# A hedgehog linear-attention and SwiGLU block: a rewrite with TensorE transposes, token-major q and k, kv summed on the fly, a folded output sum and one order of TensorE work

## Chip, cores, metric

One core of a Trainium2 chip. The metric is the device time of one execution in microseconds (us), lower is better. Engines are named as in the profile: PE is TensorE (PEld its weight loads), DVE VectorE, ACT ScalarE, POOL GpSimd, SP the engine that issues most DMAs.

## The reference, cut

```python
# x: 2048 tokens x 640, bf16; 32 heads of 20; FFN width 1728
q, k, v = split_heads(x @ wqkv)
pq, pk  = q @ w_phi[h], k @ w_phi[h]                # per head, 20 x 20
phi_q   = concat(softmax(pq), softmax(-pq))         # 40 features per head
phi_k   = concat(softmax(pk), softmax(-pk))
kv      = sum over tokens of phi_k^T v              # 40 x 20 per head
z       = sum over tokens of phi_k                  # 40 per head
a       = (phi_q @ kv / (phi_q @ z + 1e-6)) @ wo
b       = (silu(x @ w_gate) * (x @ w_up)) @ w_down
g       = sigmoid((x * gate_w).sum(-1))
out     = g * a + (1 - g) * b
```

q needs kv and z of all tokens, so the k side must end before any attention output. The FFN depends on nothing of this and can fill TensorE meanwhile. Both kernels first multiply wq and wk by w_phi, so that pq and pk are one product each.

## The kernel before, the parts that matter

A helper records every operation, keeps for each address range who wrote and read it last, and emits the semaphore waits. It also makes an engine wait for its own earlier instruction where ranges conflict; a PSUM address counts as its whole bank.

```python
def req(ev):                      # in run(): what an instruction must wait for
    ...
    s, v = ev
    if v > need.get(s, 0):
        need[s] = v               # also where s is the engine's own semaphore
...
for c in range(5):                # x and wq, wk are transposed by the DMA
    dma("sp", xT[:, c, :], x2[:, c * P:(c + 1) * P], transpose=True)
...
def tile_k(t):                    # token-major: 128 tokens x 640
    mm_group(p1(b, "pk0"), [(xT[:, c, tok], wqk[:, 1, c, 0:512]) for c in range(5)])
    mm_group(p1(b, "pk1"), [(xT[:, c, tok], wqk[:, 1, c, 512:D]) for c in range(5)])
    # ACT: exp(+), exp(-); DVE: sums, reciprocals; POOL: scale. ek kept for all tokens
...
def kv_group(c, sg):              # after all k tiles: 12 groups of 16 matmuls, 126 columns
    pairs = [(ek[:, sg, t, 120 * c:120 * c + nr], v1[:, t, 126 * c:126 * c + ncol]) for t in range(NT)]
...
def zw_groups(bt, buf):           # normaliser sums, q feature-major: 8 groups of 6 matmuls, one bank
    for u in range(4):
        for sg in range(2):
            oap = ps[0:P, c0: c0 + 64]
            ...
            mm_group(oap, pairs)
...
def u_loop(bt, buf):              # 512 tokens: wo into its own banks, w_down into others
    mm_group(bank(ab0, 0, 512), pairsa0)        # 6 chunks
    mm_group(bank(ab1, 0, P), pairsa1)
    mm_group(bank(4, 0, 512), pairs0)           # 14 chunks
    mm_group(bank(5, 0, P), pairs1)
    actop(aga, a_ap, ACTF.Copy, scale=gcol)     # g * a
    dveop(...)                                  # (1 - g) * b + that
```

The normalising factors of q are worked out token-major, transposed on PE, and spread to features again by 48 further matmuls of 512 columns.

The softmax here doesn't subtract the row's maximum and nothing guards it: scores larger than these inputs give would overflow.

## Time and profile before

The median is 377.19 us (377.03 to 378.57, 4 runs). The profiled execution spans 376.0 us.

First the busy table of the page of the kernel before (engine, busy us, share of the span, instructions), then the two lines of its chain of work that ended last (shares of the span by engine, then by line).

```profile
PE 340.0 (90%) x2164; PEld 178.1 (47%) x2201; DVE 139.2 (37%) x258; ACT 156.9 (42%) x290; POOL 127.9 (34%) x153
PE 84%; ACT 4%; SPq 3%; DVE 3%; issue 2%; DMA 2%; POOLq 0%; POOL 0%
PE ps L310 83%; SPq L297 3%; DMA xT<-in_A_x_dram 2%; ACT eq L325 2%; DVE ksum L471 1%; DVE hT L621 1%; PE pst L316 1%; ACT hT L325 1%; ACT oT L325 1%; ACT wqk L325 0%; ACT us L325 0%; POOLq L797 0%; DVE krec L472 0%; POOL hT L624 0%; DVE ocomb L661 0%
...
```

PE is what the kernel waits for. How close it is to its own limit is read from the timeline, where each line is a start, a length, the engine, the operation, the shape and a count; a length can reach past the next start (1.24 us from 93.81, the next start at 94.89), so rates are read from start to next start. The view of the kernel before, PE only:

```profile
92.04 1.93 PE L310 MATMUL ps<-v_55,ek 128*120 128x126 bf16 x32
93.81 1.24 PE L310 MATMUL ps<-xT,wg 128*128 128x512 bf16 x5
94.89 1.24 PE L310 MATMUL ps<-xT,wu 128*128 128x512 bf16 x5
...
174.84 3.22 PE L310 MATMUL ps<-SZW,eq 120*128 120x64 bf16 x48
178.12 1.02 PE L310 MATMUL ps<-xT,wg 128*128 128x512 bf16 x4
```

Five matmuls of 512 columns take 1.08 us (93.81 to 94.89), 216 ns each. The 32 of 126 columns take 1.77 us, 55 ns each. Columns / 2.4 GHz + 2.5 ns fits both (215.8 and 55.0 ns). It is a fit to these timings, and the streamed times below are estimates made with it. The 48 normaliser matmuls of 64 columns take 3.28 us, 68 ns each, where that sum gives 29: here something holds PE.

The waits of PE in the kernel before, longest first (total, times, longest):

```profile
PE ps L310 <- DMA xT<-in_A_x_dram: 20.0, 1, 20.0
...
```

By the program's own count PE streams 764,112 columns in 2,201 matmuls: 318.4 us for the columns and 5.5 for the 2.5 ns each, 324 us. The other 52 us of the span are no work of PE.

### The profile page before, as it was taken

The page shows a single profiled execution, that of the slowest core. Times are in us where ns is not written, and L with a number is a line of the kernel's source. Part 1 is how long each engine was busy: PE and PEld are TensorE (multiplying, and loading weights), DVE is VectorE, ACT ScalarE, POOL GpSimd, SP SyncE. Part 2 cuts the span into 40 slices and gives each one's busy share as a digit, 9 for nine tenths or more (in the row PEclk, how much of TensorE's full clock was granted, in tenths as well). Part 3 has the DMA queues.
Part 4 walks back from the last instruction along what each step waited for, and adds up shares of the span by engine and source line. Part 5 has one row for each costly group of instructions (what it writes and reads, how often), then busy time and mean ns, then how long its engine had stood idle before and what let it go on. Part 6 is the DMA issues. An engine that isn't in the chain of part 4 may idle for free.

```text
span 376.0 us, 5517 instructions
## 1 busy us (share of the span) xinstructions
PE 340.0 (90%) x2164; PEld 178.1 (47%) x2201; DVE 139.2 (37%) x258; ACT 156.9 (42%) x290; POOL 127.9 (34%) x153
## 2 busy tenths in 40 slices
PE   0088899999999998999999999999999999999996
PEld 0044455557654543554444455444445554444454
DVE  1000898883321580112772201157420111782211
ACT  0134666672357445113537213634551154436210
POOL 4970698784262120003333200214340012333200
PEclk9999999999999999999999999999999999999999
DMA  8968766200000000000000011000000100000011
GB/s 181 186 133 184 244 169 187 61 0 2 2 0 2 0 2 0 30 24 21 0 0 1 2 37 35 0 2 0 2 0 19 35 17 2 1 2 0 2 35 37
DMA packets 29510, 15.54 MB, mean 41 GB/s; under 512 B 19309, under 2 KB 29485, under 8 KB 29485
## 3 DMA queue, kind: packets, MB, share of 16 engines
q1 hardware_dynamic: 27097, 14.34, 15.5%
q10 hardware_dynamic: 1812, 0.83, 1.0%
q8 instruction: 18, 0.29, 0.3%
q0 software_dynamic: 576, 0.01, 0.1%
q14 instruction: 7, 0.06, 0.0%
HBM read 8.30 MB, written 2.62 MB: 29 GB/s over the span
## 4 chain that ended last, share of the span: by engine, by line
PE 84%; ACT 4%; SPq 3%; DVE 3%; issue 2%; DMA 2%; POOLq 0%; POOL 0%
PE ps L310 83%; SPq L297 3%; DMA xT<-in_A_x_dram 2%; ACT eq L325 2%; DVE ksum L471 1%; DVE hT L621 1%; PE pst L316 1%; ACT hT L325 1%; ACT oT L325 1%; ACT wqk L325 0%; ACT us L325 0%; POOLq L797 0%; DVE krec L472 0%; POOL hT L624 0%; DVE ocomb L661 0%
## 5 line engine op out<-in xcount | busy, mean ns | idle before, releaser
L624 POOL TENSOR_TENSOR hT<-hT,us 128x512 bf16<-128x512 bf16 (+1 forms) x56 | 64.3, 1151 | 200.0 <-DVE hT L621 104.6
L621 DVE SCALAR_TENSOR_TENSOR hT<-hT,ps 128x512 bf16<-128x512 bf16 (+1 forms) x56 | 38.0, 684 | 86.6 <-ACT hT L325 86.6
L310 PE MATMUL ps<-xT,wu 128*128 128x512 bf16 (+1 forms) x273 | 69.0, 379 | 0.4
L310 PE MATMUL ps<-xT,wg 128*128 128x512 bf16 (+1 forms) x269 | 67.3, 379 | 2.0 <-DVE hT L621 1.1
L310 PE MATMUL ps<-wd,hT 128*128 128x128 bf16 (+1 forms) x440 | 62.5, 297 | 1.2 <-POOL hT L624 0.9
L325 ACT ACTIVATE hT<-ps 128x512 bf16<-128x512 f32 (+1 forms) x56 | 33.3, 595 | 49.5 <-PE ps L310 49.5
L310 PEld LDWEIGHTS ps<-wd,hT 128*128 128x128 bf16 x448 | 35.0, 98 | 27.2 <-POOL hT L624 0.8
L474 POOL TENSOR_TENSOR ek<-ek,krec 128x640 bf16<-128x640 bf16 x32 | 39.7, 1268 | 19.0 <-ACT ek L325 14.6
L310 PE MATMUL ps<-wvg,xT 128*128 128x500 bf16 (+1 forms) x160 | 26.2, 316 | 20.9 <-DMA xT<-in_A_x_dram 20.0
L661 DVE SCALAR_TENSOR_TENSOR ocomb<-ps,gs,ag 128x640 bf16<-128x640 f32 x16 | 14.1, 884 | 82.6 <-PE ps L310 82.6
L325 ACT ACTIVATE us<-ps 128x512 bf16<-128x512 f32 (+1 forms) x56 | 33.5, 598 | 26.5 <-PE ps L310 26.1
L310 PEld LDWEIGHTS ps<-xT,wu 128*128 128x128 bf16 (+1 forms) x280 | 27.0, 99 | 32.4 <-issue 2.8
L310 PEld LDWEIGHTS ps<-xT,wg 128*128 128x128 bf16 (+1 forms) x280 | 25.9, 98 | 31.1 <-PE ps L310 2.9
L325 ACT ACTIVATE ag<-ps,gs 128x640 bf16<-128x640 f32 x16 | 12.7, 793 | 62.4 <-PE ps L310 62.4
L471 DVE TENSOR_REDUCE ksum<-ek 128x32 f32<-128x640 bf16 x32 | 25.1, 783 | 36.1 <-ACT ek L325 36.1
L325 ACT ACTIVATE eq<-ps 120x512 bf16<-120x512 f32 (+1 forms) x48 | 26.0, 593 | 20.8 <-PE ps L310 20.5
L588 DVE TENSOR_TENSOR eq<-eq,ps 120x512 bf16<-120x512 bf16 (+1 forms) x48 | 30.7, 681 | 3.6 <-PE ps L310 3.4
L310 PE MATMUL ps<-wo,oT 120*128 120x512 bf16 (+3 forms) x188 | 28.6, 297 | 1.3 <-ACT oT L325 0.7
L310 PE MATMUL ps<-xT,wqk 128*120 128x512 bf16 (+1 forms) x120 | 29.3, 380 | 0.2 <-DVE hT L621 0.2
L310 PEld LDWEIGHTS ps<-wvg,xT 128*128 128x128 bf16 x160 | 14.3, 102 | 32.2 <-issue 22.4
L325 ACT ACTIVATE ek<-ps 128x640 bf16<-128x640 f32 x32 | 20.8, 701 | 11.4 <-PE ps L310 11.3
L310 PE MATMUL ps<-wqk,xT 128*128 128x128 bf16 (+1 forms) x154 | 23.2, 296 | 1.1 <-ACT wqk L325 0.8
(59 smaller groups left out, 246.6 us busy)
## 6 DMA issues: line engine op xcount, KB each, us to landing
out_dram<-ocomb SPq DMA_DIRECT2D x16, 160.0 KB, 1.8
wg<-in_B_w_gate_dram SPq DMA_DIRECT2D x4, 540.0 KB, 3.8
wu<-in_B_w_up_dram SPq DMA_DIRECT2D x4, 540.0 KB, 3.9
wd<-in_B_w_down_dram SPq DMA_DIRECT2D x1, 2080.0 KB, 13.3
wvg<-in_A_wqkv_dram ACTq DMA_DIRECT2D x1, 800.0 KB, 6.8
wo<-in_A_wo_dram SPq DMA_DIRECT2D x1, 750.0 KB, 6.8
wbd<-in_A_w_phi_dram ACTq DMA_DIRECT2D x14, 0.8 KB
wbd<-in_A_w_phi_dram POOLq DMA_DIRECT2D x14, 0.8 KB, 6.1
```

The lines of the kernel that those rows point to most:

```text
L297: return eobj.dma_start(dst, src, transpose=True)
L310: last = pe.matmul(out_ap, lhsT=l, rhs=r, start=(i == 0), stop=(i == n - 1))
L316: return pe.transpose(out_ap, in_ap, ident[:, :])
L325: return act.activation(out_ap, in_ap, func, scale=scale)
L471: dveop(lambda eka=eka, sa=sa: dve.tensor_reduce(sa, eka, AX.X, ALU.add), [eka], [sa])
L474: poolop(lambda eka=eka, rb=rb: pool.tensor_tensor(eka, eka, rb, ALU.mult), [eka, ra], [eka])
L588: dveop(lambda ea=ea, oap=oap: dve.tensor_tensor(ea, ea, oap, ALU.mult), [ea, oap], [ea])
L621: dveop(lambda hap=hap, gap=gap: dve.scalar_tensor_tensor(out=hap, in0=hap, scalar=1.0, in1=gap, op0=ALU.add, op1=ALU.mult), [hap, gap], [ ...
L624: poolop(lambda hap=hap, usa=usa: pool.tensor_tensor(hap, hap, usa, ALU.mult), [hap, usa], [hap])
L661: dveop(lambda oc=oc, b_ap=b_ap, omg=omg, aga=aga: dve.scalar_tensor_tensor(out=oc, in0=b_ap, scalar=omg, in1=aga, op0=ALU.mult, op1=ALU.add),
```

## The change

The intent: fewer columns through PE, and PE never waiting. The new kernel is a rewrite; the core of the diff, with cuts:

```diff
@@ the helper: PE no longer waits for itself
+            if s == eng and not dma and (eng == "pe" or not raw):
+                return
...
@@ inputs: plain loads, transposed on PE, copied out by DVE
-    for c in range(5):
-        dma("sp", xT[:, c, :], x2[:, c * P:(c + 1) * P], transpose=True)
+    def xpose(t0, n):
+        ...
+            transposes([(o[:, c * P:(c + 1) * P], xs[:, t % 6, c * P:(c + 1) * P]) for c in range(5)])
+            copy("dve", xT[:, t, :, :].rearrange("p c k -> p (c k)"), o)
...
@@ the v weights first, the gate's column of 640 elements after them into the same tile
+    dma("act", wvg[:, :, 0:D], wv_src)
+        dma("pool", wvg[:, :, D:D + 1], bass.AP(gate_w.tensor, gate_w.offset, [[1, P], [P, 5], [1, 1]]))
...
@@ kv: one tile after the other into two banks that stay open, 11 chunks of 3 heads x 2 signs
+    def kvtile(t):
+        for j in range(NCH):
+            o = bank(bk, 63 * jj, 63 * jj + 63, 0, 120)
+            pairs.append((o, ekr[:, b, 120 * j:120 * j + 120], v1r[:, b, 63 * j:63 * j + 63], ...))
...
@@ q token-major; normalisers by DVE; the scaled features transposed by the DMA
-    def zw_groups(bt, buf):        # and zw_ops, zw_transposes, exp_psi_item
+    def qtile(t):
+        pr = tok_proj(t, 0)
+        head_exps(pr, e)
+        def vec():                 # nine vector operations, recorded one item later
+            reduce(qz[:, s, :], e.rearrange("p (g d) -> p g d", d=DH))
+            tt("dve", ez[:, s, :], e, zb[:, 0:1280], ALU.mult)
+            reduce(qw[:, s, :], ez[:, s, :].rearrange("p (g d) -> p g d", d=DH))
+            ...                    # five small ones, up to the factors qc, times g / (1 - g)
+            tt("pool", ...)        # ph = eq * qc
+            dma("sp", phiT[:, (t // 4) % 2, t % 4, :, :], ph[:, b, :], transpose=True)
+        defer(1, vec)
+    def oitem(bt, part):           # 64-row products in pairs: partitions 0 to 63, and 64 to 127
+                    l, o = kvsb[0:120, j, :], bank(2 * pr + i, 0, 512, 64 * s, 64 * s + 64)
...
@@ w_down and wo in one accumulation, scaled once by 1 - g
+        ls = [(hT[:, buf, k, tok], wd[:, k, :]) for k in range(13)]
+        ls += [(hT[0:104, buf, 13, tok], wd[0:104, 13, :])]
+        ls += [(oT[:, buf, m, tok], wog[:, m, :]) for m in range(5)]
+        actop(o.rearrange("p (b c) -> p b c", b=2), halves(pr), ACTF.Copy, omg[:, t:t + 1])
...
@@ every piece of PE work gets a place in one order; each takes the next of 3, later 4, pairs of PSUM banks
+    for u in range(4):
+        put(NT + 3.65 + 1.6 * u, qtile, u)
+    todo.sort(key=lambda z: z[:2])
```

The items also put the instructions for DVE, ACT and POOL into the program, so the order of items is the order of their instructions too.

## The prediction

> **What bounds the kernel now.** TensorE. The page's busy table has PE at 340 of 376 us; the chain of waits puts 83% of the span on it. The timeline gives its rate: groups of five 128x512 matmuls start 1.08 us apart (216 ns each), 32 of 126 columns take 1.77 us (55 ns each), 28 alternating 512/128 3.80 us. That is columns/2.4 GHz + 2.5 ns[...]; weight loads never show as a limit. The program streams 764,000 columns in 2,205 matmuls: 318 + 6 = 324 us (estimate). The other 52 us: PE waits 20.0 us for transposed x; 3 us of tail (fused DVE op, output DMA); about 29 us of holes: the first k tiles waiting for ACT and DVE (37 to 46 us), normaliser groups of six 64-column matmuls that wait for each other in one bank (3.3 us per block against 1.5 streamed), small PE transposes, ACT waits at 142 to 146 us.
>
> **What the change does to PE.** Gone, in columns: normaliser sums (12k), expansion of the factors (25k), padding of the q projection (10k) and of wo (10k), dense premultiply (24k, becomes 7k), kv at 126 columns (21.5k, becomes 11k), half-empty FFN chunks (10k). Down-projection and wo share one accumulation: 5.16 us per token tile against 5.44. Added: 130 transposes of 128 columns (17k), a 1.3k broadcast. New total 683,000 columns in about 2,040 matmuls: 285 + 5 = 290 us, 34 us less, all on the critical path. Two terms are uncertain by 4 us each: the 63-column kv matmuls may be held by their 120-column weight loads (at most 55 ns, against 29 streamed), and the paired 64-row output matmuls in different array halves may overlap ([...]no run here yet shows it).
>
> **Start.** x arrives untransposed. But the first v tile needs the gate column, whose DMA waits for all of wv and goes through POOL's queue (before: wv 6.8 us, small POOL DMAs 6 us to landing). I expect the first v matmul at 11 to 12 us and the first k matmul near 24 (36.9 before). PE still loses about 14 us there.
>
> **Other engines.** ACT stays near 160 us. DVE grows from 139 to about 175: 48 reductions of 1280 (about 1.4 us, from 783 ns for 640), about 4.7 us per q tile in all. POOL: 128 to about 150 (1280-wide scaling, about 2.5 us). None passes PE. Vector work of q delays the FFN's DVE op by up to 5 us, about what four PSUM pairs hide. 16 DMA transposes have 15 us of slack. The last four x tiles queue behind all FFN weights and land near 54 us, needed near 51: 0 to 5 us lost.
>
> **Sum.** 290 + 2 (terms above) + 14 start + 2 cold clock + 3 tail + 6 holes = **317 us**, range **308 to 331**. Faster by over 2%: 0.96; within 2%: 0.03; slower: 0.01.
>
> **Right or wrong shows in:** PE busy about 300; first v matmul at 11 to 12 us; no PE wait over 1 us between 60 us and the end; five-matmul FFN groups still 1.08 us apart; down group 5.16 us.
>
> **Wrong if:** PE waits for DVE in the q stretches (325 and up); kv or transposes run above 60 ns; x tiles 12 to 15 arrive late; the granted clock falls under 0.9; or the start is under 8 us (310).

The rate is the fit above. That weight loads are no limit is what the chain of the kernel before shows: PEld is on none of its lines, though busy for 47% of the span. The 2 us for the cold clock have their measure in the same trace: the 500-column v matmuls of the kernel before start about 415 ns apart from 20.0 to 24.3 us, and 211 ns apart from there on; 4.3 us at about half the rate lose about 2 us (estimate). The 15 us of slack of the DMA transposes is the author's estimate; in the new kernel one took 3.5 us from issue to landing (median of 16).

## The result and the profile after

326.12 us median (325.45 to 327.81, 4 runs) against 377.19 us. The ratio is 0.8646, 95% interval 0.8619 to 0.8672. Ratios here and below are the mean time of one kernel's fast runs over that of the other's of the same rounds, so not quite the ratio of the medians quoted.

The profiled execution of the new kernel is the slowest of the four (327.81 us; its span of 326.1 us is close to the median of the device times only by accident, the other three spans are 323.7 to 324.6). Its mean clock is 0.990, that of the others 0.995 or 1.0. So the sums below, which are made on this span, hold about 2 us that the other executions don't have.

Of the new kernel, the busy table and the chain of the page:

```profile
PE 301.0 (92%) x2041; PEld 182.5 (56%) x2041; DVE 177.5 (54%) x266; ACT 151.4 (46%) x254; POOL 153.4 (47%) x117
PE 80%; DVE 9%; ACT 4%; DMA 4%; POOL 1%; issue 1%; POOLq 0%
PE ps L252 79%; DMA wvg<-in_gate_w_dram 2%; DVE qw L291 2%; DVE qz L291 2%; DVE ez L280 2%; DMA wvg<-in_A_wqkv_dram 2%; PE ps L264 2%; POOL ekr L280 1%; DVE hT L284 1%; DVE ksum L291 1%; ACT wqk L270 1%; ACT ekr L270 1%; ACT eq L270 1%; DVE qd L294 0%; ACT v1r L270 0%
...
```

PE still leads, but DVE now has 9% of the chain. The waits of PE in the new kernel:

```profile
PE ps L264 <- DMA xs<-in_A_x_dram: 7.0, 4, 3.4
PE ps L252 <- DVE hT L284: 6.4, 4, 2.5
PE ps L252 <- DMA wvg<-in_gate_w_dram: 2.8, 1, 2.8
PE ps L252 <- POOL ekr L280: 2.3, 2, 1.5
...
```

The waits for x and the gate are the start. The 6.4 us for DVE were not in the forecast's sum in that size. The timeline of the new kernel, PE only, at the first v tiles, the first k tiles, a kv group, the q stretch and one steady output tile:

```profile
12.67 4.38 PE L252 MATMUL ps<-wvg,xT 128*128 128x320 bf16 x20 [2.82 <-DMA wvg<-in_gate_w_dram]
16.89 0.72 PE L264 MATMUL ps<-ident,xs 128*128 128x128 bf16 x10
...
26.19 4.45 PE L252 MATMUL ps<-wqk,xT 128*128 128x320 bf16 x20 [1.30 <-ACT wqk L270]
30.47 0.44 PE L264 MATMUL ps<-ident,wqn 128*128 128x128 bf16 x5
...
43.77 0.74 PE L252 MATMUL ps<-v1r,ekr 128*120 128x63 bf16 x11
44.35 1.53 PE L252 MATMUL ps<-wvg,xT 128*128 128x320 bf16 x10
...
125.63 1.25 PE L252 MATMUL ps<-xT,wg 128*128 128x512 bf16 x5 [2.50 <-DVE hT L284]
...
141.71 1.67 PE L252 MATMUL ps<-phiT,kvsb 120*64 120x512 bf16 x7 [1.85 <-DVE hT L284]
143.31 2.30 PE L252 MATMUL ps<-xT,wg 128*128 128x512 bf16 x5
...
160.88 3.97 PE L252 MATMUL ps<-wd,hT 128*128 128x320 bf16 x28
164.68 1.52 PE L252 MATMUL ps<-wog,oT 128*128 128x320 bf16 x10
166.04 1.24 PE L252 MATMUL ps<-xT,wg 128*128 128x512 bf16 x5
...
179.93 1.05 PE L252 MATMUL ps<-phiT,kvsb 120*64 120x512 bf16 x8
180.92 1.25 PE L252 MATMUL ps<-xT,wt 128*128 128x512 bf16 x5
```

Read from start to start: an output tile takes 5.16 us (160.88 to 166.04), exactly its 38 matmuls of 320 columns at full rate. A kv group of 11 takes 0.58 us (43.77 to 44.35), 53 ns for 63 columns that would stream in 29. Twenty v matmuls take 4.22 us at the start (12.67 to 16.89) where full rate is 2.72: the trace has them 267 ns apart up to 15.6 us and 136 ns apart from 15.8, so the clock is not yet up. Twenty matmuls of the first k tile take 4.28 us (26.19 to 30.47), again 267 ns apart up to 29.4 us and 136 from there. PE waits 2.50 and 1.85 us for DVE before 125.63 and 141.71, and five matmuls at 143.31 take 2.1 us (to the next start, not shown) in place of 1.08: after the second wait the clock fell. The trace's record of the granted clock has two such drops in this execution, 25.98 to 29.40 and 142.04 to 145.45 us, 3.4 us each at half.

Why the longer wait left the clock alone and the shorter one did not, the record does not show. In this execution its changes lie at 3, 4, 37, 38 and 91 times 3.413 us from its first entry (15.74 us). Cut into such stretches, the wait of 1.85 us lay whole in one (138.62 to 142.04), and the clock was at half in the next; the wait of 2.50 us (123.13 to 125.63) was cut by the border at 124.97 into 1.84 and 0.66. But PE was busy 1.57 us in the stretch before the drop and also 1.57 us in that from 121.56 to 124.97, after which none came. And in the reordered run (run 5) the same wait of 1.85 us, 139.39 to 141.24, left the clock alone: the five matmuls after it take 1.09 us (142.38 to 143.47), and the mean clock is 1.000. So the length of the wait does not decide it alone; a threshold is not shown.

The windows view of the new kernel (stretch, its length, then busy us and instruction count of PE, PEld, DVE, ACT and POOL, granted clock, DMA share, GB/s), for the q stretch and one after it:

```profile
103.00:146.00 43.00, 37.55 (x190) 17.80 (x188) 39.69 (x56) 25.20 (x42) 29.15 (x18) 0.96 0.21 40
146.00:200.00 54.00, 54.00 (x334) 31.71 (x332) 23.52 (x37) 23.41 (x38) 21.83 (x16) 1.00 0.15 35
```

From 146 us to the last matmul PE has no listed wait. In the q stretch DVE is busy 39.7 of 43 us.

### Where the 51 us came from

"Streamed" is columns / 2.4 GHz + 2.5 ns a matmul by the program; "lost until the first k matmul" is its start less what PE streamed before it (36.90 less 12.76; 26.19 less 10.09).

| | before | new |
|---|---|---|
| streamed | 323.9 | 289.9 |
| lost until the first k matmul | 24.1 | 16.1 |
| after the last matmul | 3.0 | 3.6 |
| everything else | 25.0 | 16.5 |
| span | 376.0 | 326.1 |

Two thirds of the gain are columns not streamed (34 us), 8 us the start. Of "everything else" before, the first run below shows that some 10 us were PE waiting for itself.

### The profile page after: what moved, and what is told of

Read it like the earlier page. It is cut to its first block, busy times and chain, and to the rows that moved or that the text cites. A ratio compares the mean times of both kernels' runs of the same rounds, so it can differ in the third digit from the quotient of the medians.

```text
span 326.1 us, 4990 instructions
## 1 busy us (share of the span) xinstructions
PE 301.0 (92%) x2041; PEld 182.5 (56%) x2041; DVE 177.5 (54%) x266; ACT 151.4 (46%) x254; POOL 153.4 (47%) x117
## 4 chain that ended last, share of the span: by engine, by line
PE 80%; DVE 9%; ACT 4%; DMA 4%; POOL 1%; issue 1%; POOLq 0%
PE ps L252 79%; DMA wvg<-in_gate_w_dram 2%; DVE qw L291 2%; DVE qz L291 2%; DVE ez L280 2%; DMA wvg<-in_A_wqkv_dram 2%; PE ps L264 2%; POOL ekr L280 1%; DVE hT L284 1%; DVE ksum L291 1%; ACT wqk L270 1%; ACT ekr L270 1%; ACT eq L270 1%; DVE qd L294 0%; ACT v1r L270 0%
## 5 line engine op out<-in xcount | busy, mean ns | idle before, releaser
L252 PE MATMUL ps<-xT,wg 128*128 128x512 bf16 x260 | 65.7, 384 | 4.0 <-DVE hT L284 3.6
L280 POOL TENSOR_TENSOR ph<-eq,qc 128x1320 bf16<-128x1320 bf16 x16 | 38.8, 2425 | 58.9 <-DVE qc L533 58.9
L252 PE MATMUL ps<-xT,wu 128*128 128x512 bf16 x260 | 64.6, 379 | 0.0
L270 ACT ACTIVATE hT<-ps 128x512 bf16<-128x512 f32 (+2 forms) x60 | 35.8, 596 | 60.0 <-PE ps L252 55.9
L252 PE MATMUL ps<-wd,hT 128*128 128x320 bf16 x448 | 63.5, 299 | 0.0
L280 POOL TENSOR_TENSOR ekr<-ekr,krec 128x1280 bf16<-128x1280 bf16 x16 | 37.6, 2357 | 34.5 <-DVE krec L294 34.5
L252 PE MATMUL ps<-wqk,xT 128*128 128x320 bf16 x320 | 50.1, 306 | 2.0 <-ACT wqk L270 1.3
L252 PEld LDWEIGHTS ps<-xT,wu 128*128 128x128 bf16 x260 | 25.5, 98 | 31.0 <-issue 0.6
L252 PEld LDWEIGHTS ps<-wqk,xT 128*128 128x128 bf16 x320 | 31.4, 100 | 17.4 <-ACT wqk L270 1.5
L270 ACT ACTIVATE osb<-ps,omg 128x640 bf16<-128x640 f32 x16 | 12.7, 793 | 60.8 <-PE ps L252 60.8
L270 ACT ACTIVATE ekr<-ps 128x640 bf16<-128x640 f32 x32 | 22.5, 703 | 16.6 <-PE ps L252 16.1
L252 PE MATMUL ps<-wvg,xT 128*128 128x320 bf16 (+1 forms) x160 | 25.8, 311 | 2.9 <-DMA wvg<-in_gate_w_dram 2.8
```

The source lines that it names most:

```text
L252: last = pe.matmul(o, lhsT=l, rhs=r, start=st, stop=sp_, skip_group_check=sk)
L270: return run("act", lambda: act.activation(o, i, func, scale=scale), rd, [o])
L280: return run(e, lambda: eo.tensor_tensor(o, a, b, op), [a, b], [o])
```

## The experiments

Twelve kernels ran. The first undoes nothing but adds one thing to the kernel before; the others start from the new kernel. The kernel before ran in the rounds, with medians of 377.61, 377.94 and 378.04 us on three chips. The new kernel did not run in these: a difference from its 326.12 us is one across chips, and where it is small the ratios to the kernel before, 0.8646 for the new kernel, are the fairer comparison.

### 1. The kernel before without PE waiting for itself

```diff
             s, v = ev
+            if s == eng == "pe":
+                return
             if v > need.get(s, 0):
```

> The kernel before, with one thing of the new one: TensorE no longer waits on its own earlier instruction (groups that write the same PSUM bank one after the other go out without a wait). Theory 1 (most of the gain is fewer streamed columns, the waits of TensorE on itself are the 7 us of the normaliser groups): the 48 normaliser matmuls of a block go from 3.3 us to about 1.5 us, the time from 377 to 369 us. Theory 2 (the gain comes from the order and the synchronisation): 377 to 355 us or less. If the 64-column groups are held by something else than the wait, they stay at 3 us and the time at 376 or 377.

367.83 us (4 runs), ratio 0.9742 (0.9725 to 0.9759), correct. The timeline of this run, PE only:

```profile
172.57 1.60 PE L312 MATMUL ps<-SZW,eq 120*128 120x64 bf16 x48
174.23 1.03 PE L312 MATMUL ps<-xT,wg 128*128 128x512 bf16 x4
```

The 48 matmuls now take 1.66 us in place of 3.28. The four transposes of a block take 0.35 us in place of 1.08. Four blocks of both make 9.4 us of the 9.8 gained. Theory 1 holds: a needless wait of an engine on itself cost the kernel before 10 us, and two lines would have had that gain, a fifth of the whole. (2.9 of the 9.4 us are the transposes, which the forecast of this run had not named.)

### 2. x transposed by the DMA again

The five transposing loads of the kernel before, xT laid out as there, no PE transposes of x.

```diff
+    for c in range(5):
+        dma("sp", xT[:, c, :], x2[:, c * P:(c + 1) * P], transpose=True)
-    put(-10, xpose, 0, 2)              # and all other xpose items and loads of xs
```

> The new kernel with x transposed by the DMA as in the kernel before (80 TensorE transposes and their 16 DVE copies fall away, x comes as five transposing loads). Theory 1 (the early start is worth more than the 4.5 us that the transposes cost TensorE): the first v matmul goes from 12.7 to about 20.3 us, the first k matmul from 26.2 to about 33 us, the sum is about 3 to 5 us slower, 330 us. Theory 2 (the start is set by the other loads and by ACT and DVE): the same time or faster by up to 4 us, 322 to 326 us.

333.94 us (4 runs), ratio 0.8844 (0.8811 to 0.8876), correct, 7.8 us slower than the new kernel. Its waits of PE:

```profile
PE ps L252 <- DMA xT<-in_A_x_dram: 22.6, 1, 22.6
PE ps L252 <- DVE hT L284: 4.6, 3, 2.5
PE ps L252 <- POOL ekr L280: 3.9, 2, 3.1
...
```

The first v matmul came at 22.6 us, 9.9 later than in the new kernel, the first k matmul at 36.8, 10.6 later. The sum was to have been 3 to 5 us: I had put the first v matmul at 20.3. Direction and mechanism hold, the size is larger. The PE transposes pay for themselves: 80 of 56 ns are 4.5 us of PE, a quarter of it before the first v matmul, where PE would wait anyway; the other 60 stand among later work.

### 3. The output sum taken apart

wo's chunks into a PSUM pair of their own, ACT scales, DVE adds, as before.

```diff
-        ls += [(oT[:, buf, m, tok], wog[:, m, :]) for m in range(5)]
+        la = [(oT[:, buf, m, tok], wog[:, m, :]) for m in range(5)]
+        pa = next_pair()               # 10 matmuls into pair pa, then
+        actop(ga..., halves(pa), ACTF.Copy, omg[:, t:t + 1])
-        actop(o..., halves(pr), ACTF.Copy, omg[:, t:t + 1])
+        stt(o..., halves(pr), omg[:, t:t + 1], ga..., ALU.mult, ALU.add)
```

> The new kernel with the output accumulation taken apart as in the kernel before: wo's five chunks into a PSUM pair of their own, ACT scales them to SBUF, DVE adds them to the scaled down-projection. The columns streamed are the same. Theory 1 (folding buys nothing of its own on TensorE, its gain is only the smaller padding): the time within 1.5 us of 326. Theory 2 (the extra pair of banks and 16 more DVE operations of 0.9 us bring waits): 3 us or more slower.

331.72 us (4 runs), ratio 0.8770 (0.8744 to 0.8796), correct, 5.6 us slower. Theory 2: from 146 us on, where the new kernel has no wait of PE, this one waits 3.2 us for DVE and 0.6 for ACT. The rest of the 5.6 us is not assigned. The waits of PE in this run over the whole span:

```profile
PE ps L253 <- DVE hT L285: 9.0, 7, 2.5
PE ps L253 <- ACT oT L271: 0.6, 2, 0.3
...
```

So the fold saves no column here, and is still worth about 5 us (4.7 by the ratios): it frees a pair of banks per output tile and 16 operations of DVE. Which of the two counts was not separated.

### 4. The kv weights padded to 128 columns

```diff
-            o = bank(bk, 63 * jj, 63 * jj + 63, 0, 120)
-            pairs.append((o, ekr[:, b, 120 * j:120 * j + 120], ...
+            o = bank(bk, 63 * jj, 63 * jj + 63)
+            pairs.append((o, ekr[:, b, 120 * j:120 * j + 128], ...
```

> The new kernel with the kv weights padded from 120 to 128 columns (the 8 extra output rows are never read). In the new kernel 11 kv matmuls of 63 columns take 0.58 us, 53 ns each, against 29 streamed. Theory 1 (the 120-column weight load is the limit; loads of 128 columns are faster): 0.32 to 0.36 us a group, 16 groups, about 4 us less, 322 us. Theory 2 (a matmul of few columns has a floor of its own near 53 ns): 0.58 us as now, 326 us.

323.98 us (4 runs), ratio 0.8575 (0.8545 to 0.8605), correct. The timeline of this run, a group and what follows:

```profile
43.45 0.50 PE L252 MATMUL ps<-v1r,ekr 128*128 128x63 bf16 x11
43.79 1.52 PE L252 MATMUL ps<-wvg,xT 128*128 128x320 bf16 x10
```

0.34 us in place of 0.58: 31 ns each against 29 streamed. Theory 1 holds. The loads themselves differ in the same way: in the new kernel one of 120 columns takes 135 ns and one of 128 takes 97 to 107. Of the 3.8 us saved on PE 2.1 reached the median (2.7 by the ratios). PE's waits for POOL and DVE grew by 0.5 us together (2.3 to 2.6 and 6.4 to 6.6); what is left is within the noise.

### 5. The 64-row output products: reordered, and all in one half

In the reordered run the loops over sign and chunk were swapped, so that two products for the same half follow each other; in the other all went to partitions 0 to 63.

```diff
-        for i, m in enumerate(ms):
-            for s in range(2):
+        for s in range(2):
+            for i, m in enumerate(ms):
```

> The new kernel with the output products reordered: two matmuls into partitions 0 to 63, then two into 64 to 127, in place of alternating. In the new kernel 8 of them (512 columns, 64 rows of output) take 0.99 us, 124 ns each, against 216 streamed. Theory 1 (neighbours in different halves of the array run at the same time): only one pair of the four in each group can overlap, 8 take about 1.3 to 1.6 us, the time grows by about 1.5 us. Theory 2 (a 64-row matmul is simply faster): 0.99 us still.

```diff
-                    l, o = kvsb[0:120, j, :], bank(2 * pr + i, 0, 512, 64 * s, 64 * s + 64)
+                    l, o = kvsb[0:120, j, :], bank(2 * pr + i, 0, 512, 0, 64)
```

> The new kernel with every 64-row output product written to PSUM partitions 0 to 63 (wrong on purpose: the second of each pair overwrites the first). In the new kernel and in the reordered one the trace has these matmuls start in pairs, 3 and 7 ns apart, the pairs 216 ns apart. Theory 1 (two products run at once because they use different halves of the array's columns): the pairs are gone, each starts 216 ns after the last, 8 take about 1.75 us in place of 0.99, about 3 us more in all. Theory 2 (a product of 64 rows is fast by itself): still 0.99 us.

One execution each: 325.84 us, correct, and 328.70 us, wrong. The timeline of the reordered run, then of the one-half run, eight products and the next matmul:

```profile
177.97 1.06 PE L252 MATMUL ps<-phiT,kvsb 120*64 120x512 bf16 x8
178.96 1.25 PE L252 MATMUL ps<-xT,wt 128*128 128x512 bf16 x5
```

```profile
178.24 1.91 PE L252 MATMUL ps<-phiT,kvsb 120*64 120x512 bf16 x8
180.09 1.25 PE L252 MATMUL ps<-xT,wt 128*128 128x512 bf16 x5
```

The reordered eight take 0.99 us as in the new kernel, and that looked like theory 2. The one-half run refutes it: 1.85 us for eight, up to 240 and mostly 216 ns apart, one after the other. So the gain is the overlap of two halves of the array, and my number for the reordered run was wrong because the order within a group does not matter. The starts in the trace, one by one, show it (us from the span's start, four matmuls of each run):

```
new kernel      179.934  179.937  180.174  180.177
reordered       177.969  177.976  178.209  178.216
one half        178.243  178.483  178.698  178.914
```

In the reordered program the first two are for the same half, yet a pair starts 7 ns apart. The trace doesn't name halves, so that a product for the other half went ahead is inferred here; a start out of program order is shown outright in the one-half run: of a group of three, the last in the program is the only one for the other half, and it started at 181.279 us, 0.23 us before the one that precedes it in the program (181.513). That the products of one half would be held by their PSUM bank and not by the array is ruled out: the second and third of the one-half run go to different banks and are still 215 ns apart. Overlap is worth 0.75 us a block, 3 us in all, which agrees with the 2 to 3 us between the one-half run and the new kernel.

### 6. The q chain on DVE in two parts

```diff
             tt("dve", ez[:, s, :], e, zb[:, 0:1280], ALU.mult)
-            reduce(qw[:, s, :], ...)
+            defer(1, vec2)
+        def vec2():                    # one item of the order later
+            reduce(qw[:, s, :], ...)   # and the rest of the chain
```

> The new kernel with the nine vector operations of a q tile handed to DVE in two parts, with the vector operation of an FFN chunk between them. TensorE waits 6.4 us for DVE between 97 and 142 us, of which 5.5 in the q stretch, and the clock falls after it. Theory 1 (an FFN operation is stuck behind a whole q chain of 5 to 6 us: an order question): the waits fall below 2 us and the time by 4 to 6 us, to 321 us. Theory 2 (DVE is simply full in this stretch, 6.1 us of chain and 2.5 FFN operations for each 6.75 us of TensorE work): the waits stay within 1.5 us of 5.5, the time within 2 us of 326.

324.65 us (4 runs), ratio 0.8618 (0.8579 to 0.8657), correct. The waits of PE between 100 and 147 us, of this run and then of the new kernel:

```profile
PE ps L252 <- DVE hT L284: 1.9, 2, 1.1
PE ps L252 <- ACT eq L270: 1.7, 1, 1.7
```

```profile
PE ps L252 <- DVE hT L284: 5.5, 3, 2.5
```

The wait for DVE fell to 1.9 us, as theory 1 says, but 1.7 us for ACT came in its place, and the time is 1.5 us lower, within what theory 2 allows. The run decides for neither.

### 7. The q tiles further apart

```diff
-        put(NT + 3.65 + 1.6 * u, qtile, u)
+        put((19.65, 21.6, 23.55, 27.9)[u], qtile, u)
-            put(a + SL * (0.22 + 0.12 * u), qtile, 4 * s + u)
+            put((31.6, 35.2, 37.0, 38.6)[u] if s == 1 else a + SL * (0.22 + 0.12 * u), qtile, 4 * s + u)
             # and the output products of blocks 0 and 1, and the output tiles of block 0, later to match
```

> The new kernel with the first eight q tiles set further apart in the order (about three FFN chunks from one q tile to the next in place of two to two and a half), and the output products of the first blocks moved back to match. The order inside DVE is as in the new kernel. Theory 2 of the split run (DVE is full: one q chain takes it 6.1 us, an FFN chunk 0.65 us; TensorE needs 1.36 and 2.16 us; the two balance at about 3.1 chunks for each q tile) : the waits of TensorE for DVE between 102 and 145 us fall from 5.5 us to under 1.5 us although the order is unchanged, the clock stays up, and the time falls by 4 to 6 us, to 321 us. Theory 1 (the order alone): the waits stay above 3 us, the time within 2 us of 326.

323.16 us (4 runs), ratio 0.8542 (0.8517 to 0.8567), correct. The same window as above in this run:

```profile
103.00:146.00 43.00, 41.43 (x213) 19.83 (x211) 36.17 (x56) 25.07 (x44) 28.70 (x19) 1.00 0.18 34
```

PE is busy 41.4 of the 43 us (37.6 before this edit), DVE 36.2 (39.7), and the granted clock is 1.00 (0.96). PE's wait for DVE in the stretch is 1.5 us, once. This profile is of the fastest of the four executions (321.66 us); the others had a mean clock of 0.992 to 0.995, so the clock did not stay up in all. The edit also moved output products and output tiles, which was not separated. The order within a q chain is the same, so theory 2 carries most of it: DVE was full. The sum shows it too. The timeline of DVE in the new kernel, from one FFN operation over one q chain to the next two:

```profile
106.66 0.81 DVE L280 TENSOR_TENSOR ez<-eq,zb 128x1280 bf16<-128x1280 bf16 x1
...
111.55 1.48 DVE L291 TENSOR_REDUCE qz<-eq 128x64 f32<-128x1280 bf16 x1
112.95 1.79 DVE L280 TENSOR_TENSOR ez<-eq,zb 128x1280 bf16<-128x1280 bf16 x1
114.77 1.49 DVE L291 TENSOR_REDUCE qw<-ez 128x64 f32<-128x1280 bf16 x1
...
117.62 1.28 DVE L284 SCALAR_TENSOR_TENSOR hT<-hT,ps 128x512 bf16<-128x512 bf16 x2
```

From 111.55 to 117.62 the chain takes 6.1 us, and two to three FFN operations of 0.65 follow: about 7.7 us for each q tile. PE needs for the same q tile and 2.5 FFN chunks 1.36 + 2.5 x 2.16 = 6.8 us. By this estimate DVE falls behind by 0.9 us a tile until the four pairs of banks are all waiting for it; six chains start in quick succession between 105 and 142 us. Part of the chain's length is POOL: the multiplication of 1280 elements takes 0.81 us at 106.66, when POOL has no work, and 1.79 at 112.95, when POOL runs FFN products at the same time; its mean is 1.21. So the two slow each other down, by an amount that varies: at 215.28 the multiplication took 1.28 us with POOL at work all the while (213.45 to 217.57), and POOL's own product took 1.73 us at 215.84, where one alone took 1.15 at 103.82. What they contend for, and what sets the amount, the traces do not show.

### 8. The gate column first, as 640 elements

```diff
+        dma("act", gcol[:, :, :], bass.AP(gate_w.tensor, gate_w.offset, [[1, P], [P, 5], [1, 1]]))
     dma("act", wvg[:, :, 0:D], wv_src)
-        dma("pool", wvg[:, :, D:D + 1], ...)
+    copy("act", wvg[:, :, D:D + 1], gcol[:, :, :])
-    put(-9, xpose, 2, 2)
+    put(-8.35, xpose, 2, 2)            # and three DVE memsets later
```

> The new kernel with the gate column loaded first into a tile of its own (no wait for the v weights), the w_phi load no longer behind it, three large memsets of DVE moved behind its first copies, and the second pair of x transposes behind the first two v tiles. Theory 1 (the start is held by the chain v weights, gate column, w_phi): the first v matmul goes from 12.7 to 6.5 to 7.5 us, the first k matmul from 26.2 to 20 to 21 us, the time falls by 5 to 6 us, to 320.5 us. Theory 2 (the start is bound by the loads' bandwidth and ACT): the first k matmul stays above 24 us and the time above 324 us.

325.84 us (4 runs), ratio 0.8625 (0.8596 to 0.8655), correct: no gain. The first v matmul came at 11.2 us, the first k matmul at 26.3 as before. The v weights needed 8.2 us to land where they had needed 5.3 in the new kernel, with nothing ahead of them on the queue. ACT's table load of 1.28 us came behind their landing, at 9.58 us, and so in front of the copy that the first v matmul needs; and the twenty v matmuls, 1.4 us earlier, took 5.20 us to the next start in place of 4.22. The edit moved the wait and did not remove it.

### 9. The gate as five rows, turned by PE

```diff
+    dma("act", grow[0:5, :], gate_w.rearrange("(c p) -> c p", p=P))
     dma("act", wvg[:, :, 0:D], wv_src)
+        run("pe", lambda: pe.transpose(o, grow[0:5, :], ident[0:5, 0:5]), ...)
+        copy("act", gcol[:, :], o)
+        copy("act", wvg[:, :, D:D + 1], gcol[:, :].unsqueeze(2))
```

> The new kernel with the gate loaded as five rows of 256 bytes (not 640 elements of 2 bytes) and turned by one small TensorE transpose, the w_phi load freed from waiting, three DVE memsets moved back, the second pair of x transposes behind the first v tiles. The first try, with the 640 elements ahead of the v weights on the same queue, had the v weights land at 9.6 us in place of 6.1 and the first v matmul at 11.2. Theory 1 (those 640 elements held the v weights back): the v weights land by 7 us, the first v matmul runs at 7 to 8 us, the first k matmul at 21 to 23 us, the time near 322 us. Theory 2 (loads share a bandwidth limit, or the first k matmul hangs on the chain of ACT and cold TensorE): the first k matmul stays at 25 us or later, the time above 324.5 us.

323.92 us (4 runs), ratio 0.8561 (0.8523 to 0.8598), correct. The timeline of this run, PE only:

```profile
8.44 5.48 PE L252 MATMUL ps<-wvg,xT 128*128 128x320 bf16 x20 [3.43 <-ACT wvg L270]
13.74 1.29 PE L264 MATMUL ps<-ident,xs 128*128 128x128 bf16 x20
```

The v weights landed in 6.6 us, the first v matmul ran at 8.4, the first k matmul at 23.6. Between the theories: 4.2 us earlier at v, 2.6 at k, 2.2 in the time. The edit has the other changes of run 8 too (the w_phi load, the memsets, the second pair of transposes), so against run 8 only the way of the gate column differs: of the 2.8 us between the two first v matmuls (11.2 and 8.4) 1.6 are the landing and 1.3 the table load, which here ran at 2.98 us, ahead of everything. That the 640 elements held the v weights back fits (8.2 us behind them in one profile; 6.6, 7.0 and 6.0 behind the five rows in runs 9, 10 and 11).

### 10. The same, with PE kept at work from the beginning

```diff
+    def dummies(n):                    # never read; three times 16, between the first loads
+        mm([(bank(KV0, 0, P), ident[:, :], ident[:, :], True, True, True) for _ in range(n)])
```

> The same with 48 matmuls of the identity by itself, never read, between the first loads, so that TensorE is at work from 1.8 us on. In the new kernel the first two v tiles take 4.2 us and the first two k tiles 4.3 us, against 2.7 at full rate. Theory 1 (those are slow because TensorE's clock is not yet up after idling): the first two v tiles take 2.7 to 3.2 us, the first k matmul comes 1.5 us or more earlier than in the run without, the time falls by 1.5 to 3 us. Theory 2 (they are slow for want of operands): no change.

322.00 us (4 runs), ratio 0.8513 (0.8484 to 0.8541), correct. The timeline of this run, PE only, the first two v tiles and what follows:

```profile
8.88 2.89 PE L252 MATMUL ps<-wvg,xT 128*128 128x320 bf16 x20 [0.98 <-ACT wvg L270]
11.61 1.28 PE L264 MATMUL ps<-ident,xs 128*128 128x128 bf16 x20
```

Twenty v matmuls in 2.73 us, full rate, where run 9 needed 5.3 (8.44 to 13.74). Theory 1 holds by the trace: with PE at work before them they start 136 ns apart, without it 265. The first k matmul came at 21.5 us, and 1.9 us reached the median, though the intervals of the two ratios overlap. The slow rate lasted about 5.3 us from the first v matmul in run 9 (all twenty of them) and about 5.9 us from the first dummies in this run (estimate: the first two sixteens are listed with 1.89 and 1.91 us, the third, from 6.30, with 1.60, so some five of the third went at the full 56 ns). The page of the new kernel shows a granted clock of 9 tenths from its first slice, because the clock record's first entry is at 15.7 us: before that, only the spacing of matmuls tells.

### 11. All together

The start of run 10, the padded kv weights, the q tiles further apart, the chain in two parts.

> All together: this start, kv weights padded to 128 columns, q tiles set further apart, q chain in two parts on DVE. If the parts add (2.1 + 3.0 + 1.5 of which spread and split overlap by half + start 4 to 6), 314 to 317 us. If the time won at the start is lost again in the k stretch (waits for POOL and DVE, later x loads behind the FFN weights), 318 to 320 us.

311.68 us (311.07 to 312.55, 4 runs), ratio 0.8246 (0.8221 to 0.8270), correct. This beats both kernels. The busy table of its page:

```profile
PE 297.5 (96%) x2090; PEld 182.0 (59%) x2090; DVE 171.8 (55%) x266; ACT 151.4 (49%) x256; POOL 151.5 (49%) x116
```

The single gains on the medians were 2.1, 3.0, 1.5 and 4.1 us, 10.7 in all; together they made 14.4, on another chip and with the kernel before 0.8 us slower there. That they add to more than their sum is not shown: by the ratios the single gains make 12.7 us and all together 15.1, and the difference of 2.4 has an uncertainty of about 3.9 (estimate from the intervals). PE's waits for DVE are 1.1 us over the whole of this run (6.4 in the new kernel, 2.8 with the split alone, 2.4 with the spread alone); what the new start and the padding add to that was not separated.

## Why the prediction was right, and where it was short

The range of 308 to 331 held 326.12, and the direction and main cause were right; the point, 317, was 9 us short.

- **Columns streamed, 324 to 290 us.** Right: 683,496 columns in 2,041 matmuls in the trace, 289.9 us. Groups of five still 1.08 us apart, output tile 5.16 us, PE busy 301.0 (forecast: about 300).
- **The two uncertain terms, +2 us.** About right as a sum, by luck in part: the forecast named two risks of 4 us in opposite directions, and both came. kv is held by its 120-column loads (53 ns, 4.3 us in all, run 4 shows the cause), the 64-row products overlap (3 us less, run 5 shows the cause).
- **Start, 14 us lost and 2 for the cold clock.** Right as a sum, 16.1 us, though each event came later: first v matmul at 12.7 us (11 to 12 forecast), first k matmul at 26.2 (24). That the sum came out is luck in part. Runs 8 to 10 took it apart: gate load, then clock.
- **The last four x tiles.** No wait; the forecast's 0 to 5 us was 0.
- **Other engines.** DVE 177.5 us (175), POOL 153.4 (150), ACT 151.4 (160). Totals right, and of no use: DVE's share of 54% hides a stretch at 92%.
- **Holes, 6 us.** This is the term that failed in size. The table's "everything else" is 16.5 us; less the 1.3 of the two terms above, 15.2. The listed waits of PE after the first k matmul make 9.8 (6.4 for DVE, 2.3 for POOL, 0.7 and 0.4 for ACT), and two drops of the clock, 3.4 us at half rate each, cost up to 1.7 us each. About 2 us are not assigned.
- **The step behind it: "Vector work of q delays the FFN's DVE op by up to 5 us, about what four PSUM pairs hide."** The delay of one chain was nearly right (5.2 to 6.2 us, 4.7 forecast), the conclusion was not. Four pairs hide one delay; they don't hide six in quick succession, each leaving DVE further behind (about 0.9 us by the estimate of run 7). The check to make was DVE's load for each q tile against PE's in that stretch, which needs only the durations that the forecast already had. Run 7 shows it.
- **"No PE wait over 1 us between 60 us and the end."** Wrong: three, 1.11, 2.50 and 1.85 us, all for DVE. They were on the forecast's list of what would make it wrong ("PE waits for DVE in the q stretches (325 and up)"): that case came true at 326.12 us, which the range still held.
- **What the forecast lacked.** It put the normaliser's self-waits at about 7 us among 29 of holes and never priced the change of the helper. Run 1 shows 9.8 us.

## What to carry to other kernels

Where PE streams at its full rate, count columns first; that gave two thirds of this gain. Then compare engines stretch by stretch, not over the span: an engine busy for half of the span can still set the pace where its work is dense, and setting that work further apart in the order cost nothing here and gave 3 to 4 us (run 7). And look whether an engine waits for itself, and what the first big product waits for: here the first cost 10 us and the second gave 8, where the folded sum gave about 5 and the paired products 3.
